# Talking-heads attention in float32: scores mixed whole instead of in parts, the second mixing matrix scaled on GpSimd, value products in two bursts a tile

## Chip, core and metric

The kernel runs on one core of a Trainium2 chip, in one launch. TensorE (PE) multiplies into PSUM, VectorE (DVE), ScalarE (ACT) and GpSimd (POOL) do elementwise work, and SyncE (SP) issues nearly all the DMAs. The five run their own instruction streams in order and meet at semaphores. The metric is device time in microseconds (us) of one execution, lower is better; the number of a kernel is the median of its runs.

## What is computed

Attention over 4 batches, 12 heads, 448 tokens and 64 features a head, in which the heads are mixed before and after the softmax, then a gated feed-forward layer and a top-1 mixture of eight experts. All is float32. The change touches the attention alone:

```python
scores = scale * np.matmul(q, k.transpose(0, 1, 3, 2))
scores = np.einsum('bhij,hg->bgij', scores, w_pre)
scores = scores - np.max(scores, axis=-1, keepdims=True)
attn = np.exp(scores)
attn = attn / (np.sum(attn, axis=-1, keepdims=True) + 1e-09)
attn = np.einsum('bhij,hg->bgij', attn, w_post)
return np.matmul(attn, v)
# then the gated layer and the experts on the tokens' rows
```

## The kernel before

The attention has 16 tiles, four of 110, 110, 110 and 120 query rows for each batch. A tile is cut into blocks of ten query rows, 11 or 12 to a tile and 180 in all. A block holds ten rows of twelve heads, so 120 partitions, with 448 keys along each. The main loop in `attention` makes one turn a block, from n = -8 on, and in each turn every stage works on another block. Per block the stages are:

- `fetch` (L233): two DMAs on SP gather the block's rows out of the tile's scores S into `xm`, eight turns ahead.
- `high` and `low` (L241, L248): `xm` is split into two float32r parts, `xh` (rounded, mostly on DVE) and the rest (mostly on POOL, at 27 blocks on DVE). The first ten blocks (`NATIVE`) are not split.
- `premix` (L254): PE mixes the heads of the block, in three float32r products (L260 to L262), or in one full float32 product for the first ten (L257). PSUM tile `psm`, three buffers.
- `peak` (L264): DVE takes each row's negated maximum `nm` (L267), ACT the exponential `e` and its row sums (L270).
- `norm` (L273): DVE adds a small number to the sums (L276), inverts them (L279) and scales the second mixing matrix K2 by them, which gives `kk` (L282).
- `post` (L286): PE mixes the weights, four full float32 products with `e` as weights and `kk` streamed (L290), into `pso`, two buffers.
- `evac` (L293): ACT (in one turn of 45 DVE) copies `pso` to the tile's weights `AT` (L298).

Between these lie, in the same turns, the scores of the next tile (`qk`, twelve heads a tile, two float32r products each, L230, copied out of PSUM by ACT at L231), the products of the last tile's weights with the values (`av`, L301: twelve halves a tile, spread by the table `AV` over nine of its turns, L318; two halves are sixteen instructions in the trace, and DVE copies the result out at L320), and the low parts of queries and keys on POOL (L204).

Beside the attention, `conv_steps` rounds the float64 weights of the gated layer to float32 for later: 72 pieces of 128x384, each with a load `f` (L123), five DVE steps (L134, L137, L140, L144, L149), one addition on POOL (L127) and a store (L146). `convert` spreads these steps evenly over the turns: 0.41 pieces a turn.

A full float32 product stands in the trace as two PE instructions and a float32r product as one. The order on each engine is the order of the code (`manual_schedule`). The gated layer starts on PE when the attention's products are through.

Of the kernel before, what the change touches and what calls it, by code (L numbers as in the profile page):

```python
"""Talking-heads attention, a gated feed-forward layer and a top-1 mixture of experts, one launch.

Large float32 products run as single-pass products of float32r parts (x = hi + lo, 12 bits each), the others in full;
the float64 weights come in as their bits and are rounded to float32 on the chip.
"""
# [6 lines left out]
F32 = mybir.dt.float32  # L12
F32R = mybir.dt.float32r
# [10 lines left out]
U = 448                      # tokens of a unit of the gated layer  # L24
CAP = 264                    # rows of an expert in the static part; the rest goes through a loop
TS = CAP // 3
OVB = 12                     # blocks of 128 rows that an expert may have beyond CAP
STR = -(-(CAP + 128 * OVB) // 16) * 16   # rows of an expert in the routing table
ITS = [(0, 110, 11), (110, 110, 11), (220, 110, 11), (328, 120, 12)]  # query rows: start, count, blocks
ORDERED = {mybir.EngineType.PE, mybir.EngineType.DVE, mybir.EngineType.Activation, mybir.EngineType.Pool, mybir.EngineType.SP}  # L30
# The attention's turns: a block of ten query rows enters in each and passes a stage in each. A batch has 45.
TURNS = 45
LA, HA, LO = 8, 6, 5         # turns that a block is fetched ahead, and its two parts made ahead, of its last stage
NATIVE = 10                  # blocks that are mixed in full float32, while the parts' engines prepare the keys
HIGH_ACT, HIGH_LAST = (35, 40), 186   # turns of a batch, and all from the last on, whose high parts ScalarE makes
LOW_DVE = (9, 18, 21, 25, 26, 33, 39)   # turns whose low parts VectorE makes
OPER_DVE = (27, 30, 37, 38, 41)   # turns in which VectorE makes a low part of the queries or keys
EVAC_DVE = (10,)             # turns in which VectorE takes the mixed weights out of PSUM
QK = [0, 1, 2, 3, 3, 5, 5, 6, 7, 8, 9, 10]   # turn of a tile's fetches in which a head of the next tile is multiplied
QK0 = [2, 2, 4, 4, 4, 5, 5, 5, 6, 6, 6, 7]   # the same for the first tile  # L40
QL = [0, 3, 6, 7]            # turns in which the queries after those are loaded
QL0 = [4, 6, 7, 8]
KL = [21, 23, 24, 29, 31, 35]   # turns of a batch in which the next one's keys are loaded
K0 = [1, 6, 7, 9]            # turns in which the first batch's later keys are prepared
VL = [(0, 7), (0, 9), (0, 9), (0, 9)]   # tile and turn of a batch's last stages in which its values are loaded
V0 = [4, 5, 9, 16]
AV = [1, 1, 2, 2, 3, 5, 6, 6, 7, 7, 9, 10]   # turns in which the last tile's weights are multiplied with the values
LGS = [2] * 12 + [4, 4]      # how the logits of a unit are spread over the products of the next
AHEAD = 3                    # tiles of weights that are loaded ahead
LOW_W = {0} | {k for k in range(200) if k % 3 == 2 and not 18 < k < 72}   # tiles of weights whose low parts VectorE makes  # L50
PARTS = ((3, 7), (4, 7), (5, 7))   # an expert's second products after which a part of its rows goes out
GATHER = [2, 2, 1, 1, 0, 0]  # chunks of the next expert's rows that are transposed beside them
CV = 384                     # elements a partition of a piece of the float64 conversion


# ------------------------------------------------------------------ host layout
# [53 lines left out]
# ------------------------------------------------------------------ float64 bits -> float32  # L110
def conv_steps(nc, pool, wx, wf):
    """Generator: rounds CV x 128 float64 numbers at a time to float32 (to nearest even), in five steps."""
# [5 lines left out]
    for i in range(len(spots) + 2):  # L118
# [9 lines left out]
        if now:  # L128
            lo, hi = raw[i - 1][:, :, 0], raw[i - 1][:, :, 1]
            a = pool.tile([128, CV], U32, name="cva", bufs=3)  # L130
            e = pool.tile([128, CV], U32, name="cve", bufs=2)
            ef = e.bitcast(F32)
            # The high word as a float32 times 2^-112 has the float32 exponent three places to the right.
            V.tensor_scalar(out=a.bitcast(F32), in0=hi.bitcast(F32), scalar1=2.0 ** -112, scalar2=None, op0=ALU.mult)  # L134
# [19 lines left out]
# ------------------------------------------------------------------ attention  # L154
def attention(tc, qa, ka, qt, kt, vt, k1, k2, xT, wx, wf):
    nc = tc.nc
    with ExitStack() as ctx:
        P = pools(tc, ctx)
        kr, kp, qr, qp, sp, cst, vp, xm, xs, ep, at, sm, xo, cv = (P(n, b) for n, b in (
            ("kr", 3), ("kp", 6), ("qr", 4), ("qp", 4), ("sp", 4), ("acst", 1), ("vp", 7), ("xm", 6), ("xs", 4), ("ep", 3), ("at", 2), ("asm", 4), ("xo", 1), ("cv", 2)))  # L160
# [4 lines left out]
        K1H = cst.tile([120, 120], F32R, name="K1H")  # L165
        K1L = cst.tile([120, 120], F32R, name="K1L")
# [7 lines left out]
        def load_k(b, g):  # L174
            if b:
                r = kr.tile([128, 2, S], F32, name="kraw")
            else:                # where a tile's weights go later
                r = spare[:, 2 * g * S:2 * g * S + 2 * S].rearrange("p (h s) -> p h s", s=S)
            RAW["k", b, g] = r
            nc.sync.dma_start(out=r, in_=kt[b, :, 2 * g:2 * g + 2, :])  # L180
# [6 lines left out]
        def prep_k(b, g):       # heads 2g, 2g + 1: hi in the upper 64 rows, lo in the lower  # L187
# [12 lines left out]
        def oper_low():         # a low part that waits, a turn after its high part at the earliest  # L200
            n = now["n"]
            if LATER and LATER[0][0] <= n:
                _, c, r, a = LATER.pop(0)
                (nc.vector if n % TURNS in OPER_DVE else nc.gpsimd).tensor_tensor(out=c, in0=r, in1=a.bitcast(F32), op=ALU.subtract)  # L204

        def prep_q(t, hf):      # three heads: hi and lo, twice
# [34 lines left out]
        def high(n):  # L241
            if n < NATIVE:
                return
            a = xs.tile([120, S], F32R, name="xh")
            (nc.scalar.copy if n % TURNS in HIGH_ACT or n >= HIGH_LAST else nc.vector.tensor_copy)(a, XS[n])  # L245
            XS[n] = a, XS[n]

        def low(n):  # L248
            if n < NATIVE:
                return  # L250
            a, x = XS[n]
            (nc.vector if n % TURNS in LOW_DVE else nc.gpsimd).tensor_tensor(out=x.bitcast(F32R), in0=x, in1=a.bitcast(F32), op=ALU.subtract)  # L252

        def premix(n):  # L254
            ps = PS[n] = pm.tile([120, 512], F32, name="psm")
            if n < NATIVE:
                nc.tensor.matmul(ps[:, :S], K1, XS.pop(n), start=True, stop=True)  # L257
                return
            a, x = XS.pop(n)
            nc.tensor.matmul(ps[:, :S], K1H, a, start=True, stop=False)  # L260
            nc.tensor.matmul(ps[:, :S], K1L, a, start=False, stop=False)
            nc.tensor.matmul(ps[:, :S], K1H, x.bitcast(F32R), start=False, stop=True)  # L262

# [9 lines left out]
        def norm(n):  # L273
# [8 lines left out]
            nc.vector.tensor_scalar(out=kk, in0=K2, scalar1=r2, scalar2=None, op0=ALU.mult)  # L282
# [19 lines left out]
        def av(t, k):           # half k of twelve: two of the four row chunks of two heads  # L302
# [30 lines left out]
        # ---- the first two tiles' scores: full float32, the other head's rows times zeros  # L333
# [16 lines left out]
        cold = ep.tile([120, S], F32, name="e")     # a product of zeros, for the clock  # L350
# [14 lines left out]
        nc.scalar.copy(K1H, K1)  # L365
        nc.vector.tensor_tensor(out=K1L, in0=K1, in1=K1H.bitcast(F32), op=ALU.subtract)

        # ---- one block a turn, its stages in different turns
        for n in range(-LA, N + 1):
# [22 lines left out]
            if 0 <= n + 3 < N:  # L392
                premix(n + 3)
            scale = norm(n + 1) if 0 <= n + 1 < N else iter(())
            next(scale, None)
            if 0 <= n + 2 < N:
                peak(n + 2)
            if 0 <= n + LO < N:
                low(n + LO)
# [5 lines left out]
            if 0 <= n + HA < N:  # L405
                high(n + HA)
# [22 lines left out]
# ------------------------------------------------------------------ the two feed-forward layers  # L429
def feed_forward(tc, xT, wf, wg, wt, w1, w2, cs, out, x2, tab, keep):  # L430
    nc = tc.nc
    V = nc.vector
    with ExitStack() as ctx:
# [27 lines left out]
        tk = []                                          # tokens less NT  # L461
# [5 lines left out]
        first = cst.tile([TS, 3], F32, name="first")     # the first expert's tokens  # L467
        V.memset(first, float(NT))
        TB0 = cst.tile([TS, 3], I32, name="TB0")
        RS = cst.tile([112, NE], F32, name="RS")      # sums to the next free row of each expert  # L470
# [33 lines left out]
        def order(inst, earlier):       # on one engine, without a wait  # L504
# [35 lines left out]
        def logits(u, row):     # of a unit that is not the last: on VectorE, beside the next unit's products  # L540
# [317 lines left out]
```

## Time and profile before

| | |
|---|---|
| median of three runs | 1515.37 us (1512.62 to 1516.2) |
| the profiled execution, its span | 1513.0 us |
| first and last product of the post-mixing | 29.7 and 569.0 us |
| PE, DVE, ACT, POOL busy over the span | 91%, 71%, 45%, 61% |

The attention takes the first 575 us or so and the two feed-forward layers the rest. The span is the profiled execution's own time; it lies 2.4 us under the median. Busy shares over the whole span mix the attention, where DVE has hardly a gap, with the later layers, where PE has none, so each stage has to be read by itself.

### The profile page before, as it was taken

How to read it: one execution, taken by the hardware profiler on the slowest of the kernel's cores; microseconds unless marked ns; L12 is line 12 of the kernel's file. 1: busy time of each engine (PE TensorE's matmuls, PEld its weight loads, DVE VectorE, ACT ScalarE, POOL GpSimd, SP SyncE). 2: the span in 40 equal slices, each digit the busy share in tenths (PEclk: the TensorE clock that was granted, in tenths of full speed). 3: DMA queues.
4: the chain of work that ended last, by engine and by line, in shares of the span. 5: the costliest groups of instructions: out<-in, count | busy, mean ns of one | idle time of the engine just before them, and what ended most of it. 6: DMA issues, size and time to landing. Idle time of an engine off the chain costs nothing.

```text
span 1513.0 us, 25664 instructions
## 1 busy us (share of the span) xinstructions
PE 1377.2 (91%) x9270; PEld 1210.4 (80%) x9270; DVE 1066.8 (71%) x2055; ACT 675.8 (45%) x1282; POOL 918.5 (61%) x560
## 2 busy tenths in 40 slices
PE   8788997998889988999999998999898799999996
PEld 3666776776667777998888897889787699999995
DVE  4899999999999997861995199529957333333331
ACT  4566666565566554333223222322331345555541
POOL 4666677766767556564557545754563566666661
PEclk9999999999999999999999999999998899999998
DMA  7675686568667666533324332333233466656650
GB/s 245 206 219 180 192 262 202 179 194 241 209 185 223 186 209 210 179 129 134 103 101 135 111 104 103 129 108 108 94 104 102 131 201 214 207 188 208 205 181 20
DMA packets 106840, 251.30 MB, mean 166 GB/s; under 512 B 28190, under 2 KB 71294, under 8 KB 106592
## 3 DMA queue, kind: packets, MB, share of 16 engines
q1 hardware_dynamic: 102351, 237.54, 49.0%
q0 software_dynamic: 4352, 12.02, 2.7%
q8 instruction: 76, 1.25, 0.3%
q14 instruction: 61, 0.49, 0.1%
HBM read 180.00 MB, written 31.79 MB: 140 GB/s over the span
## 4 chain that ended last, share of the span: by engine, by line
PE 41%; DVE 40%; issue 9%; DMA 5%; ACT 2%; SPq 2%; POOL 1%; DVEq 0%; POOLq 0%; ACTq 0%
PE mm L502 11%; PE mm L500 11%; PE mm L501 11%; DVE e L634 6%; DVE junk L546 6%; DVE kk L282 5%; DVE nm L267 4%; DVE xh L245 3%; DMA f<-in_wx 2%; DVE cva L134 2%; PE pso L290 2%; DVE e L633 1%; DVE e L636 1%; DVE e L635 1%; DVE cve L137 1%
## 5 line engine op out<-in xcount | busy, mean ns | idle before, releaser
L490 POOL TENSOR_TENSOR wlo<-wraw,whi 128x1536 fp32r<-128x1536 f32 x108 | 383.3, 3549 | 197.8 <-ACT whi L488 181.4
L500 PE MATMUL mm<-xhi,whi 128*128 128x448 f32 (+1 forms) x960 | 325.4, 339 | 12.9 <-DVE e L635 11.1
L502 PE MATMUL mm<-xlo,whi 128*128 128x448 f32 (+1 forms) x960 | 321.5, 335 | 2.5 <-POOL xlo L521 2.5
L501 PE MATMUL mm<-xhi,wlo 128*128 128x448 f32 (+1 forms) x960 | 321.2, 335 | 0.0
L290 PEld LDWEIGHTS pso<-kk,e 120*112 120x112 f32 x1440 | 168.6, 179 | 89.5 <-ACT AT L298 49.4
L290 PE MATMUL pso<-kk,e 120*112 120x120 f32 x1440 | 186.7, 273 | 50.6 <-DVE kk L282 20.0
L488 ACT CAST whi<-wraw 128x1536 fp32r<-128x1536 f32 x136 | 200.9, 1477 | 62.2 <-PE mm L502 47.6
L500 PE MATMUL mm<-hhi,whi 128*128 128x264 f32 (+1 forms) x672 | 221.9, 330 | 7.1 <-ACT hhi L639 7.1
L252 POOL TENSOR_TENSOR xm<-xm,xh 120x448 fp32r<-120x448 f32 x143 | 180.1, 1260 | 78.4 <-DVE xh L245 49.5
L502 PE MATMUL mm<-hlo,whi 128*128 128x264 f32 (+1 forms) x672 | 219.2, 326 | 1.7 <-POOL hlo L640 1.7
L501 PE MATMUL mm<-hhi,wlo 128*128 128x264 f32 (+1 forms) x672 | 218.0, 324 | 0.0
L270 ACT ACTIVATE e<-psm,nm 120x448 f32<-120x448 f32 x180 | 114.4, 635 | 204.8 <-DVE r L279 167.6
L500 PEld LDWEIGHTS mm<-xhi,whi 128*128 128x128 f32 x960 | 181.5, 189 | 26.7 <-DVE e L635 15.3
L502 PEld LDWEIGHTS mm<-xlo,whi 128*128 128x128 f32 x960 | 181.4, 189 | 12.7 <-POOL xlo L521 3.7
L501 PEld LDWEIGHTS mm<-xhi,wlo 128*128 128x128 f32 x960 | 181.9, 189 | 9.0 <-issue 0.2
L634 DVE RECIPROCAL e<-e 128x448 f32<-128x448 f32 x48 | 141.4, 2946 | 0.7
L500 PEld LDWEIGHTS mm<-hhi,whi 128*128 128x128 f32 x672 | 129.2, 192 | 12.9 <-ACT hhi L639 8.2
L502 PEld LDWEIGHTS mm<-hlo,whi 128*128 128x128 f32 x672 | 129.1, 192 | 8.5 <-POOL hlo L640 3.5
L546 DVE CUSTOM_DVE_ANT_0 junk<-row,WT 112x768 f32<-112x768 f32 x96 | 135.0, 1406 | 0.9 <-ACT row L536 0.7
L640 POOL TENSOR_TENSOR hlo<-e,hhi 128x448 fp32r<-128x448 f32 x48 | 66.8, 1393 | 111.0 <-ACT hhi L639 111.0
L501 PEld LDWEIGHTS mm<-hhi,wlo 128*128 128x128 f32 x672 | 129.2, 192 | 4.8
L267 DVE TENSOR_REDUCE nm<-psm 120x1 f32<-120x448 f32 x180 | 109.5, 608 | 1.1 <-PE psm L257 1.1
(138 smaller groups left out, 2383.4 us busy)
## 6 DMA issues: line engine op xcount, KB each, us to landing
wraw<-wf SPq DMA_DIRECT2D x72, 768.0 KB
wraw<-in_w SPq DMA_DIRECT2D x64, 768.0 KB
xm<-S SPq DMA_DIRECT2D x360, 105.0 KB
f<-in_wx SPq DMA_DIRECT2D x72, 384.0 KB
wf<-cva SPq DMA_DIRECT2D x72, 192.0 KB
qraw<-in_qt SPq DMA_DIRECT2D x56, 180.0 KB
kraw<-in_kt SPq DMA_DIRECT2D x18, 448.0 KB
vt<-in_vt SPq DMA_DIRECT2D x16, 336.0 KB
```

Source lines behind the costliest of these rows:

```text
L252: (nc.vector if n % TURNS in LOW_DVE else nc.gpsimd).tensor_tensor(out=x.bitcast(F32R), in0=x, in1=a.bitcast(F32), op=ALU.subtract)
L267: nc.vector.tensor_reduce(out=nm, in_=ps[:, :S], axis=AX.X, op=ALU.max, negate=True)
L270: nc.scalar.activation(e, ps[:, :S], AF.Exp, bias=nm, scale=1.0, accum_out=su)
L282: nc.vector.tensor_scalar(out=kk, in0=K2, scalar1=r2, scalar2=None, op0=ALU.mult)
L290: nc.tensor.matmul(po[:, c, :120], e[:, 112 * c:112 * c + 112], kk, start=True, stop=True)
L488: nc.scalar.copy(a, r)
L490: eng.tensor_tensor(out=b, in0=r, in1=a.bitcast(F32), op=ALU.subtract)
L500: nc.tensor.matmul(ps, w[0][:, j, :], x[0], start=first, stop=False)
L501: nc.tensor.matmul(ps, w[1][:, j, :], x[0], start=False, stop=False)
L502: nc.tensor.matmul(ps, w[0][:, j, :], x[1], start=False, stop=last)
L546: V.tensor_tensor_reduce(out=jk, in0=row[j], in1=WT[:, e, :], scale=1.0, scalar=0.0, op0=ALU.mult, op1=ALU.add, accum_out=lg[:, j, e:e + 1])
L634: V.reciprocal(out=e, in_=e)
```

## The change

- `high`, `low`, the matrices `K1H` and `K1L` and the pool `xs` are gone. `premix` is one full float32 product for all 180 blocks.
- `kk` is made on GpSimd, with a second multiplication by 1.0.
- The low parts of queries and keys are all on GpSimd (`OPER_DVE` is gone; it had put six halves of keys on DVE).
- `EVAC_DVE` has four turns of 45 instead of one: 16 copies of `pso` on DVE in place of 4.
- The stages are further apart: `premix` four turns ahead of `post` (three before), `peak` three (two) and `norm` two (one). The pool of `e` has five buffers (three), that of the small tiles five (four).
- `AV` puts the value products of a tile into two turns, six halves in each.

All other lines of the diff are comments and blank lines.

```diff
-LA, HA, LO = 8, 6, 5
-NATIVE = 10
-HIGH_ACT, HIGH_LAST = (35, 40), 186
-LOW_DVE = (9, 18, 21, 25, 26, 33, 39)
-OPER_DVE = (27, 30, 37, 38, 41)
-EVAC_DVE = (10,)
+LA = 8
+MIX, PEAK, NORM = 4, 3, 2
+EVAC_DVE = (2, 10, 21, 32)
...
-AV = [1, 1, 2, 2, 3, 5, 6, 6, 7, 7, 9, 10]
+AV = [3] * 6 + [8] * 6
...
-                (nc.vector if n % TURNS in OPER_DVE else nc.gpsimd).tensor_tensor(out=c, in0=r, in1=a.bitcast(F32), op=ALU.subtract)
+                nc.gpsimd.tensor_tensor(out=c, in0=r, in1=a.bitcast(F32), op=ALU.subtract)
...
-            if n < NATIVE:
-                nc.tensor.matmul(ps[:, :S], K1, XS.pop(n), start=True, stop=True)
-                return
-            a, x = XS.pop(n)
-            nc.tensor.matmul(ps[:, :S], K1H, a, start=True, stop=False)
-            nc.tensor.matmul(ps[:, :S], K1L, a, start=False, stop=False)
-            nc.tensor.matmul(ps[:, :S], K1H, x.bitcast(F32R), start=False, stop=True)
+            nc.tensor.matmul(ps[:, :S], K1, XS.pop(n), start=True, stop=True)
...
-            nc.vector.tensor_scalar(out=kk, in0=K2, scalar1=r2, scalar2=None, op0=ALU.mult)
+            nc.gpsimd.tensor_scalar(out=kk, in0=K2, scalar1=r2, scalar2=1.0, op0=ALU.mult, op1=ALU.mult)
...
-            if 0 <= n + 3 < N:
-                premix(n + 3)
-            scale = norm(n + 1) if 0 <= n + 1 < N else iter(())
+            if 0 <= n + MIX < N:
+                premix(n + MIX)
+            scale = norm(n + NORM) if 0 <= n + NORM < N else iter(())
             next(scale, None)
-            if 0 <= n + 2 < N:
-                peak(n + 2)
-            if 0 <= n + LO < N:
-                low(n + LO)
+            if 0 <= n + PEAK < N:
+                peak(n + PEAK)
...
-            if 0 <= n + HA < N:
-                high(n + HA)
```

Lines move: L257 becomes L238, L290 L266, L318 L294, L267 L243, L282 L258, L298 L274, and the conversion's DVE steps L131, L134, L137, L141 and L146.

DVE in the middle of the attention, one turn and part of the next, before (`r` are the sums, then their inverse, `X` the value products on their way out):

```order
L276 TENSOR_SCALAR r_5600<-su 120x1
L267 TENSOR_REDUCE nm<-psm 120x1
L279 RECIPROCAL r_5608<-r_5600 120x1
L137 TENSOR_SCALAR cve<-cva 128x384
L282 TENSOR_SCALAR kk<-K_123,r_5608 120x120
L245 CAST xh<-xm 120x448
L320 COPY X<-psv 128x3x11x10
L140 TENSOR_SCALAR cva<-cva 128x384
```

And two turns with the same kind of steps in the changed kernel:

```order
L252 TENSOR_SCALAR r_5668<-su 120x1
L243 TENSOR_REDUCE nm<-psm 120x1
L255 RECIPROCAL r_5675<-r_5668 120x1
L134 TENSOR_SCALAR cve<-cva 128x384
L137 TENSOR_SCALAR cva<-cva 128x384
L252 TENSOR_SCALAR r_5696<-su 120x1
L243 TENSOR_REDUCE nm<-psm 120x1
L255 RECIPROCAL r_5703<-r_5696 120x1
L141 SCALAR_TENSOR_TENSOR cva<-f_5464,cve 128x384
```

Two DVE instructions of each turn (`kk`, `xh`) are gone. POOL at a like place, before:

```order
L127 TENSOR_TENSOR cve<-cva,cve 128x384
L204 TENSOR_TENSOR qlo<-qraw,qhi 128x360
L252 TENSOR_TENSOR xm<-xm,xh 120x448
L204 TENSOR_TENSOR qlo<-qraw,qhi 128x360
L252 TENSOR_TENSOR xm<-xm,xh 120x448
```

and in the changed kernel:

```order
L258 TENSOR_SCALAR kk<-K_120,r_3653 120x120
L124 TENSOR_TENSOR cve<-cva,cve 128x384
L199 TENSOR_TENSOR qlo<-qraw,qhi 128x360
L258 TENSOR_SCALAR kk<-K_120,r_3697 120x120
L258 TENSOR_SCALAR kk<-K_120,r_3727 120x120
L124 TENSOR_TENSOR cve<-cva,cve 128x384
```

Where a subtraction of 448 elements a partition stood, a scaling of 120 stands, and it waits for DVE's `r`. PE around value products, before:

```order
L290 MATMUL pso<-kk,e 112x120 x4
L318 MATMUL psv<-AT,vt 64x120 x4
L260 MATMUL psm<-xh,K1H 120x448
L261 MATMUL psm<-xh,K1L 120x448
L262 MATMUL psm<-xm,K1H 120x448
L230 MATMUL psq<-ks,qhi 110x448
L230 MATMUL psq<-ks,qlo 110x448
```

and in the changed kernel, a turn without value products, one with a burst and one after it:

```order
L238 MATMUL psm<-xm,K_119 120x448
L266 MATMUL pso<-kk,e 112x120 x4
L294 MATMUL psv<-AT,vt 64x110 x24
L238 MATMUL psm<-xm,K_119 120x448
L225 MATMUL psq<-ks,qhi 110x448
L225 MATMUL psq<-ks,qlo 110x448
L266 MATMUL pso<-kk,e 112x120 x4
```

One premix product stands for three, and 24 value products stand in a row.

## Rows read from the trace of the kernel before

**Rows 1.** The page: busy time of the engines, and DVE's busy tenths in 40 slices.

```profile
PE 1377.2 (91%) x9270; PEld 1210.4 (80%) x9270; DVE 1066.8 (71%) x2055; ACT 675.8 (45%) x1282; POOL 918.5 (61%) x560
...
DVE  4899999999999997861995199529957333333331
```

**Rows 2.** Busy time of each engine in a stretch, then clock, DMA share and rate.

```profile
100.00:508.00 408.00, 357.83 (x2873) 287.47 (x2872) 403.60 (x980) 248.75 (x601) 284.30 (x240) 0.99 0.68 207
```

**Rows 3.** The post-mixing's line L290: durations in ns, first and last start.

```profile
L290 PE MATMUL pso<-kk,e x1440: 263/266/514, 29.7 to 569.0; 120*112 120x120 f32 x180
```

**Rows 4.** DVE's groups in 100 to 508 us: count, busy us, mean ns, idle before.

```profile
L282 DVE TENSOR_SCALAR kk<-K,r 120x120 f32<-120x120 f32 x132 | 77.3, 586 | 0.0
L245 DVE CAST xh<-xm 120x448 fp32r<-120x448 f32 x126 | 64.9, 515 | 0.8 <-DMA xm<-S 0.7
...
L252 DVE TENSOR_TENSOR xm<-xm,xh 120x448 fp32r<-120x448 f32 x19 | 15.5, 814 | 0.0
```

**Rows 5.** The timeline of all engines around 305 us: start, duration, what.

```profile
302.80 0.27 DVE L282 TENSOR_SCALAR kk<-K,r 120x120 f32<-120x120 f32 x1
...
302.98 0.38 DVE L245 CAST xh<-xm 120x448 fp32r<-120x448 f32 x1
...
305.61 1.27 POOL L252 TENSOR_TENSOR xm<-xm,xh 120x448 fp32r<-120x448 f32 x1
...
305.79 1.17 DVE L282 TENSOR_SCALAR kk<-K,r 120x120 f32<-120x120 f32 x1
```

**Rows 6.** DVE's timeline late in the attention: two conversion steps.

```profile
562.46 0.34 DVE L137 TENSOR_SCALAR cve<-cva 128x384 uint32<-128x384 uint32 x1
...
563.84 0.54 DVE L144 SCALAR_TENSOR_TENSOR cva<-f,cve 128x384 uint32<-128x384 uint32 x1
```

**Rows 7.** PE's timeline at five places; what follows directly gives the spacing.

```profile
24.31 0.92 PE L257 MATMUL psm<-xm,K 120*120 120x448 f32 x2
25.06 2.54 PE L226 MATMUL psq<-AT 128*110 128x448 f32 x6
...
305.79 0.47 PE L260 MATMUL psm<-xh,K1H 120*120 120x448 f32 x1
...
306.50 0.37 PE L230 MATMUL psq<-ks,qhi 128*110 128x448 f32 x1
306.70 0.36 PE L230 MATMUL psq<-ks,qlo 128*110 128x448 f32 x1
307.10 1.05 PE L290 MATMUL pso<-kk,e 120*112 120x120 f32 x8
307.91 0.44 PE L260 MATMUL psm<-xh,K1H 120*120 120x448 f32 x1
...
569.97 2.68 PE L318 MATMUL psv<-AT,vt 112*64 112x120 f32 x48 [0.24 <-ACT AT L298]
572.48 2.63 PE L318 MATMUL pso<-AT,vt 112*64 112x120 f32 x48
```

**Rows 8.** POOL's groups in 100 to 508 us, as rows 4.

```profile
L252 POOL TENSOR_TENSOR xm<-xm,xh 120x448 fp32r<-120x448 f32 x114 | 144.0, 1264 | 57.4 <-DVE xh L245 39.5 <-issue 8.3 <-ACT xh L245 3.6
L127 POOL TENSOR_TENSOR cve<-cva,cve 128x384 f32<-128x384 f32 x54 | 61.9, 1146 | 25.9 <-DVE cve L149 17.6 <-PE psm L262 3.6 <-DVE r L276 3.0
...
L204 POOL TENSOR_TENSOR ks<-kraw,ks 64x448 fp32r<-64x448 f32 x26 | 32.3, 1247 | 1.7
```

**Rows 9.** SP from 100 to 508 us: the fetches, one other issue, its longest wait.

```profile
L238 SPq DMA_DIRECT2D xm<-S x266: 762/783/1183, 100.7 to 506.9; - x133
...
317.98 0.49 SPq L123 DMA_DIRECT2D f<-in_wx  x1
...
SPq L146 <- DVE r L276: 53.4, 30, 4.3
```

**Rows 10.** PE's timeline in the first turns: two premix products, two turns apart.

```profile
40.49 0.92 PE L257 MATMUL psm<-xm,K 120*120 120x448 f32 x2
...
44.86 0.92 PE L257 MATMUL psm<-xm,K 120*120 120x448 f32 x2
```

More of the change, by code (lines that the diff above doesn't have):

```diff
@@ L158, in attention @@
         P = pools(tc, ctx)
-        kr, kp, qr, qp, sp, cst, vp, xm, xs, ep, at, sm, xo, cv = (P(n, b) for n, b in (
-            ("kr", 3), ("kp", 6), ("qr", 4), ("qp", 4), ("sp", 4), ("acst", 1), ("vp", 7), ("xm", 6), ("xs", 4), ("ep", 3), ("at", 2), ("asm", 4), ("xo", 1), ("cv", 2)))
+        kr, kp, qr, qp, sp, cst, vp, xm, ep, at, sm, xo, cv = (P(n, b) for n, b in (
+            ("kr", 3), ("kp", 6), ("qr", 4), ("qp", 4), ("sp", 4), ("acst", 1), ("vp", 7), ("xm", 6), ("ep", 5), ("at", 2), ("asm", 5), ("xo", 1), ("cv", 2)))
         pq, pm, pp, pv = (P(n, b, "p") for n, b in (("pq", 2), ("pm", 3), ("pp", 2), ("pv", 1)))
@@ L164, in attention @@
         K2 = cst.tile([120, 120], F32, name="K2")
-        K1H = cst.tile([120, 120], F32R, name="K1H")
-        K1L = cst.tile([120, 120], F32R, name="K1L")
         conv = conv_steps(nc, cv, wx, wf)
@@ L239, in fetch @@
             XS[n] = x
-        def high(n):
-            if n < NATIVE:
-                return
[L244 to L252, printed above, removed]
         def premix(n):
             ps = PS[n] = pm.tile([120, 512], F32, name="psm")
-            if n < NATIVE:
-                nc.tensor.matmul(ps[:, :S], K1, XS.pop(n), start=True, stop=True)
-                return
-            a, x = XS.pop(n)
-            nc.tensor.matmul(ps[:, :S], K1H, a, start=True, stop=False)
-            nc.tensor.matmul(ps[:, :S], K1L, a, start=False, stop=False)
-            nc.tensor.matmul(ps[:, :S], K1H, x.bitcast(F32R), start=False, stop=True)
+            nc.tensor.matmul(ps[:, :S], K1, XS.pop(n), start=True, stop=True)
         def peak(n):
@@ L364, in attention @@
         nc.vector.tensor_scalar(out=K1, in0=K1, scalar1=1.0 / np.sqrt(D), scalar2=None, op0=ALU.mult)
-        nc.scalar.copy(K1H, K1)
-        nc.vector.tensor_tensor(out=K1L, in0=K1, in1=K1H.bitcast(F32), op=ALU.subtract)
         for n in range(-LA, N + 1):
```

## The prediction

> **What bounds the kernel now.** I read the page first. Over the whole span PE is busiest, but DVE's tenths stand at 9 for the first 14 slices and fall afterwards [rows 1], so the attention, where the change is made, has to be read alone. From 100 to 508 us DVE is busy 403.60 of 408 us, PE 357.83, POOL 284.30 and ACT 248.75 [rows 2]. SP issues 266 fetches there [rows 9], two a block, so 133 turns pass in 408 us: **3.07 us a turn**. PE's 357.83 is less full than it looks, because a product's duration holds its latency: in rows that follow without a wait the spacing is shorter than the duration [rows 7]. The limit is DVE. DVE's groups have next to no idle time before them [rows 4].
>
> Part of DVE's time isn't its own work. A scaling `kk` takes 0.27 us alone, but 1.17 us at 305.79 us, where a POOL subtraction has begun 0.18 us earlier: the subtraction ends at 306.88 us, `kk` at 306.96 us [rows 5]. The mean of `kk` is 586 ns and that of `xh` 515 ns against 0.38 us alone [rows 4, 5].
>
> The Trainium skill has the rule for this in "SBUF — State Buffer", section "Who interferes with whom": VectorE and GpSimd share one pair of ports, as an exclusive lock for the whole instruction, and whichever starts first blocks the other. The trace agrees in the pair just read. It is weighed below, since the change gives GpSimd a new instruction a turn.
>
> **The change part by part.** *DVE* loses `kk`, `xh` and its share of the low parts: 77.3 + 64.9 + 15.5 = 157.7 us in the middle stretch [rows 4], 1.19 us a turn. It gains twelve copies of `pso` in the whole attention, which I price like the cast of about as many elements at 0.5 us [rows 4]: 6 us, 4 of them in the middle. What is left is 403.6 - 157.7 + 4 = 250 us, **1.88 us a turn**, with the stretching of the conversion steps as it is now. Six halves of keys go from DVE to POOL, at 1.25 us each [rows 8]: 8 us.
>
> *PE* in spacings: the three-part premix takes 306.50 - 305.79 = 0.71 us, the full one 25.06 - 24.31 = 0.75 us; a turn's post-mixing 307.91 - 307.10 = 0.81 us; a score product 0.20 us; 48 value instructions in a row 572.48 - 569.97 = 2.51 us [rows 7]. A tile has 11.25 turns on average, 24 score products and two such bursts. The new turn is 0.75 + 0.81 + 24 x 0.20 / 11.25 (0.43) + 2 x 2.51 / 11.25 (0.45) = **2.44 us**. The premix by itself is 0.04 us a turn dearer, 7 us in all, and it is hidden as long as PE isn't the limit; after the change PE is.
>
> *SP*: two fetches of 783 ns, and beside them 0.41 loads and 0.41 stores of the conversion, and 106 loads and stores of queries, keys, values and results over 180 turns, at up to 0.49 us [rows 9]: 1.57 + 1.41 x 0.49 = **2.26 us a turn**, with no gap between them. The change removes none of it. SP waits long now for DVE before a conversion store, 53.4 us in 30 times [rows 9]; the fetches of the next turns stand behind that wait. A fetch now has four turns to land before its premix (before, two to its split), so a late one is forgiven more.
>
> *ACT* has 248.75 / 133 = 1.87 us a turn [rows 2] and loses the twelve copies and a few casts. *POOL* loses 144.0 us of subtractions [rows 8] and keeps 284.30 - 144.0 = 140.3 us, with the keys' halves 1.1 us a turn. It gains `kk`, of which the trace has no POOL row. The nearest rows by kind of work are the conversion's addition, 384 elements a partition in 1146 ns, and the keys' subtraction, 448 in 1247 ns [rows 8]; in proportion 120 elements are 0.36 us, and if a small instruction costs as much as the dearest row, 1.25 us. I take 0.4 us, since those two rows grow with the elements. POOL then has 1.5 us a turn. `post` needs `kk` two turns after its sums instead of one, so this stays off PE's path.
>
> *What is late next.* PE (2.44) and SP (2.26) lie close together, DVE and ACT 0.5 us below. PE doesn't reach its sum, since the engines meet every turn. The first turns show by how much: they already mix in full float32, have no `xh` and no value products yet. There PE's sum is 0.75 + 0.81 + 0.43 = 1.99 us, and the premix products at 40.49 and 44.86 us, two turns apart, give 2.19 us a turn [rows 10], 10% more. With that, 2.44 becomes 2.65 us. The middle saves 133 x (3.07 - 2.65) = **56 us**. From 29.7 to 569.0 us are 539 us [rows 3], so 47 turns lie outside the middle, in 131 us, 2.79 each. Ten of them are native already and gain little; the last 20 or so have no scores to make, and PE's sum there is near 2.0. I take 2.5 on average: **13 us**. The further stage costs one more premix before the first post-mixing, 1 us. Together 68 us: 1513.0 - 68 = 1445 us. The median of the runs shown is 2.4 us above that span, so **1447 us**. The later layers do the same work and move forward with the attention's end.
>
> **Rivals.** *PE runs full* at 2.44 us, because DVE and the further stages leave enough slack: the middle saves 84, the ends 20, and the time is 1411 us. Against it: the 10% in the first turns.
>
> *SP becomes the limit.* It issues in order, and its waits for DVE, 0.4 us a turn now, may remain, since the conversion's store still stands between the fetches. With gaps and some transfers later (the DMA share of 0.68 [rows 2] grows to 0.79 at 2.65 us a turn), 2.85 us a turn: 29 us in the middle, 6 at the ends, 1480 us. For it: a sum of 2.26 us leaves little room; against it: DVE reaches the store's step earlier.
>
> *The bursts starve the others.* During 2.51 us of value products no premix comes, and with three `psm` buffers DVE and ACT can't work far ahead. If DVE then needs 2.4 us in the 9.25 turns without a burst and the two burst turns last 2.0 + 2.5 us, a tile is 31.2 us, 2.77 a turn: 40 + 9 us saved, 1466 us. Speaking against it: DVE's 1.88 us is below PE's 2.0 in such a turn.
>
> *Slower: `kk` on GpSimd costs too much.* POOL's instructions and those of DVE that stretch beside them go partly one after the other. Before, they add up to 284.30 / 133 = 2.14 for POOL [rows 2], 0.27 and 0.36 for `kk` and `xh` alone [rows 5], and 0.41 x (3 x 0.34 + 2 x 0.54) = 0.86 for the five conversion steps [rows 6]: 3.63 us in a turn of 3.07, so 0.85 of the sum is what a turn takes. After, it is 0.85 x (1.1 + 0.86 + k) for a `kk` of k: 2.0 us at 0.4, 2.7 at 1.25, and 3.07 from k = **1.65 us** on. Beyond that the kernel is slower; at 2.0 us, which a two-step scaling with a scalar for each partition could cost, a turn is 3.37 and 180 turns are 54 us more, 1569 us. The dearest small POOL row, 1.25 us, doesn't reach the point.
>
> By the skill's rule above with no overlap at all, the sum itself would be the turn, and the point would lie at 1.1 us. The rows of before, 3.63 in 3.07, don't go so far, so I give the rule's full form a small part of the chance.
>
> **How the numbers follow.** Forecast 1447 us, with 1430 to 1460 as its own spread: 0.54. PE full, 1411: 0.13. Bursts, 1466: 0.11. SP, 1480: 0.13. `kk` at about its point, within 0.3% of now (that is about what a measurement of this kernel can tell from no change): 0.04. `kk` beyond it, 1569: 0.05. Faster is 0.91, same 0.04, slower 0.05. The range leaves out the slower and unchanged cases and the lower part of the first rival: **1415 to 1487 us**.
>
> **What would show it.** Right: premix at 0.75 us spacing in the middle, 2.6 to 2.7 us a turn, DVE with idle time before its `nm` because of PE, ACT's waits for DVE mostly gone, POOL's `kk` below 0.7 us. SP as the limit would show as fetches issued without a gap and DVE idle for `f` or PE for `xm`. Wrong would be a DVE still without idle time, or PE waiting for `kk` from POOL.

## The result, and the profile after

The changed kernel takes **1464.36 us** (median of four runs, 1461.21 to 1466.73), the kernel before on the same chip 1515.78 us: a ratio of 0.9662 with an interval of 0.9645 to 0.9679. The time is 51 us shorter, where 68 were forecast. It lies in the range of 1415 to 1487 us, 17 us above the forecast of 1447 and outside its own spread, and next to the rival in which the bursts starve the other engines (1466).

The profiled execution has a span of 1460.5 us, 52.5 less than before. Its page first: busy time by engine, and DVE's busy tenths in 40 slices.

```profile
PE 1361.3 (93%) x9100; PEld 1182.2 (81%) x9100; DVE 873.4 (60%) x1691; ACT 663.4 (45%) x1261; POOL 834.7 (57%) x603
...
DVE  3767767757666778709990799169937333333331
```

In the attention DVE stood at 9 from the third slice on [rows 1] and now stands at 5 to 7. The post-mixing's line (durations in ns, first and last start):

```profile
L266 PE MATMUL pso<-kk,e x1440: 263/266/513, 33.9 to 518.9; 120*112 120x120 f32 x180
```

And the middle of the attention, with PE, PEld, DVE, ACT and POOL busy, granted clock, DMA share and rate:

```profile
100.00:460.00 360.00, 336.59 (x2645) 257.98 (x2642) 243.44 (x686) 233.67 (x575) 206.18 (x257) 0.98 0.76 228
```

The groups of DVE and POOL in the same stretch (count, busy us, mean ns, idle before and what ended it) hold 129 `nm` and 129 `kk`, so 129 turns in 360 us, 2.79 us a turn in place of 3.07:

```profile
L243 DVE TENSOR_REDUCE nm<-psm 120x1 f32<-120x448 f32 x129 | 79.0, 612 | 0.0
L296 DVE COPY X<-psv 128x330 f32<-128x330 f32 (+1 forms) x23 | 17.4, 757 | 55.0 <-PE psv L294 54.9
L258 POOL TENSOR_SCALAR kk<-K,r 120x120 f32<-120x120 f32 x129 | 74.4, 577 | 107.9 <-DVE r L255 86.4 <-PE psq L225 17.4 <-PE psm L238 1.3
```

The difference between the two spans can be split by stage, with the 47 turns outside the middle taken as what is left over. The first post-mixing comes 4.2 us later (33.9 for 29.7). From there to the last one 539.3 us have become 485.0: 133 turns at 2.79 in place of 3.07 save 36.8 us, and the other 47 take 485.0 - 371.2 = 113.8 us in place of 131.3, 17.5 less. What follows the last post-mixing is 1460.5 - 518.9 = 941.6 us, before 944.0: 2.4 us. Together 36.8 + 17.5 - 4.2 + 2.4 = 52.5.

DVE no longer sets the pace: 243.44 of 360 us. These waits of that stretch bear on what does (who waited, for whom, us, times, longest; the last row is from SP's own list).

```profile
ACT e L246 <- DVE r L255: 86.9, 62, 5.3
DVE X L296 <- PE psv L294: 54.9, 22, 5.9
DVE cva L131 <- DMA f<-in_wx: 49.8, 30, 5.1
PE psm L238 <- DMA xm<-S: 9.3, 4, 3.1
SPq L143 <- DVE r L252: 10.3, 7, 3.8
```

Three things that the forecast's sum didn't have stand in the timelines. The first is a burst. PE, then DVE (start, duration, instruction):

```profile
169.06 0.92 PE L238 MATMUL psm<-xm,K 120*120 120x448 f32 x2
169.81 0.98 PE L266 MATMUL pso<-kk,e 120*112 120x120 f32 x8
173.11 2.68 PE L294 MATMUL psv<-AT,vt 112*64 112x120 f32 x48
175.72 1.01 PE L238 MATMUL psm<-xm,K 120*120 120x448 f32 x2
```

```profile
171.33 0.53 DVE L146 SCALAR_TENSOR_TENSOR cve<-f,cve 128x384 f32<-128x384 uint32 x1
175.84 0.79 DVE L296 COPY X<-psv 128x360 f32<-128x360 f32 x1 [3.98 <-PE psv L294]
176.79 0.61 DVE L243 TENSOR_REDUCE nm<-psm 120x1 f32<-120x448 f32 x1
```

The copy of the value products is the next instruction in DVE's order. DVE stands before it for 3.98 us, until the burst that begins at 173.11 us is done, and `nm` stands behind it, and so do the exponentials that need it.

The second comes in the turn of a batch's first value products. Before them PE waits 2.64 us for the fetch of a later block, and soon after that its products take about twice as long. PE's timeline, and the engines' busy time with the granted clock, 0.51 from 191 to 198 us, so nearly all of it at the lower level, 1.2 GHz:

```profile
189.69 1.01 PE L238 MATMUL psm<-xm,K 120*120 120x448 f32 x2 [2.64 <-DMA xm<-S]
...
191.90 1.91 PE L266 MATMUL pso<-kk,e 120*112 120x120 f32 x8 [0.78 <-POOL qlo L199]
193.74 4.54 PE L294 MATMUL psv<-AT,vt 112*64 112x110 f32 x48
198.21 1.01 PE L238 MATMUL psm<-xm,K 120*120 120x448 f32 x2
```

```profile
184.00:191.00 7.00, 4.36 (x24) 2.83 (x24) 2.24 (x8) 2.87 (x8) 2.09 (x3) 1.00 0.90 273
191.00:198.00 7.00, 6.22 (x55) 5.91 (x56) 2.59 (x6) 2.83 (x8) 2.62 (x4) 0.51 0.82 261
```

The third is the start: with one more premix ahead of the first post-mixing, PE meets a premix whose fetch hasn't landed while the next score products stand behind it, waits 3.83 us, and goes on at a granted clock of 0.63.

```profile
20.61 1.82 PE L238 MATMUL psm<-xm,K 120*120 120x448 f32 x2 [3.83 <-DMA xm<-S]
22.22 3.33 PE L221 MATMUL psq<-AT 128*110 128x448 f32 x6
```

```profile
21.00:25.00 4.00, 4.00 (x7) 1.53 (x7) 1.16 (x2) 0.75 (x2) 2.68 (x2) 0.63 0.46 128
```

### The profile page after: what moved, and what is told of

Same layout as the page of the kernel before. It is cut to its first block, busy times and chain, and to the rows that moved or that the text cites. A ratio compares the mean times of both kernels' runs of the same rounds, so it can differ in the third digit from the quotient of the medians.

```text
span 1460.5 us, 24833 instructions
## 1 busy us (share of the span) xinstructions
PE 1361.3 (93%) x9100; PEld 1182.2 (81%) x9100; DVE 873.4 (60%) x1691; ACT 663.4 (45%) x1261; POOL 834.7 (57%) x603
## 4 chain that ended last, share of the span: by engine, by line
PE 59%; DVE 19%; DMA 8%; issue 6%; ACT 2%; POOL 2%; SPq 2%; POOLq 0%; DVEq 0%; ACTq 0%
PE mm L472 12%; PE mm L470 12%; PE mm L471 12%; PE pso L266 6%; DVE e L604 6%; PE psm L238 6%; DVE junk L516 5%; DMA f<-in_wx 4%; PE psv L294 4%; PE psq L225 3%; DVE e L603 1%; SPq L233 1%; DVE e L606 1%; DMA xm<-S 1%; DVE e L605 1%
## 5 line engine op out<-in xcount | busy, mean ns | idle before, releaser
L266 PEld LDWEIGHTS pso<-kk,e 120*112 120x112 f32 x1440 | 172.1, 179 | 55.7 <-POOL kk L258 22.0
L266 PE MATMUL pso<-kk,e 120*112 120x120 f32 x1440 | 183.3, 271 | 20.0 <-ACT AT L274 9.8
L258 POOL TENSOR_SCALAR kk<-K,r 120x120 f32<-120x120 f32 x180 | 104.0, 578 | 158.1 <-DVE r L255 124.0
L238 PE MATMUL psm<-xm,K 120*120 120x448 f32 x360 | 169.9, 554 | 13.1 <-DMA xm<-S 13.1
```

The costliest lines, as they stand in the source:

```text
L258: nc.gpsimd.tensor_scalar(out=kk, in0=K2, scalar1=r2, scalar2=1.0, op0=ALU.mult, op1=ALU.mult)
L266: nc.tensor.matmul(po[:, c, :120], e[:, 112 * c:112 * c + 112], kk, start=True, stop=True)
```

## Experiments

Two questions were put. Which of the edits carries the gain? And what holds the turn at 2.79 us and the start 4 us back? The ratio of each kernel is to the kernel before, run on the same chip (its median 1514.9 to 1517.6 us).

### Which edit carries the gain

**The full float32 mixing alone**, in the kernel before: all other edits of the change are left out.

```diff
-NATIVE = 10
+NATIVE = 180
```

> The kernel before with one part of the change alone: all blocks mixed in full float32, with no parts made; kk stays on VectorE, stages and value products as before. Theory A (this part carries the gain): VectorE falls from 3.03 to about 2.3 us a turn, 1470 to 1480 us. Theory B (it takes kk's move as well): 1495 us or more, VectorE still without idle time.

Measured: 1454.39 us (1453.51 to 1460.37), ratio 0.9600 [0.9572, 0.9628]. One line gives more than the whole change, by 10 us, and more than either theory gave it. Its middle, and DVE's scaling there:

```profile
100.00:460.00 360.00, 352.93 (x2701) 264.82 (x2696) 267.81 (x829) 242.27 (x590) 129.27 (x123) 1.00 0.76 231
```

```profile
L282 DVE TENSOR_SCALAR kk<-K,r 120x120 f32<-120x120 f32 x132 | 51.0, 386 | 0.0
```

132 turns in 360 us, 2.73 us each. DVE keeps `kk` and is busy 268 of 360 us all the same: without `xh` and the subtractions on POOL, `kk` has gone from 586 ns [rows 4] to 386. PE is nearly full.

**`kk` on GpSimd alone**, in the kernel before.

```diff
-            nc.vector.tensor_scalar(out=kk, in0=K2, scalar1=r2, scalar2=None, op0=ALU.mult)
+            nc.gpsimd.tensor_scalar(out=kk, in0=K2, scalar1=r2, scalar2=1.0, op0=ALU.mult, op1=ALU.mult)
```

> The kernel before with one part of the change alone: kk on GpSimd. Theory A (VectorE's own work was the limit, so each instruction taken off it counts): VectorE loses 0.58 us a turn, 1440 to 1470 us. Theory B (VectorE and GpSimd go partly one after the other, and GpSimd's subtractions are still there): the sum of both is as before, 0.27 us off one and about 0.6 us onto the other, 1505 to 1525 us. Theory C (the post-mixing one turn after its kk is too near): slower than 1525 us.

Measured: 1514.82 us (1511.95 to 1518.15), ratio 1.0000 [0.9986, 1.0015]. No change, though DVE loses `kk`, 77.3 us of instructions in 408 us [rows 4]. DVE's busy time from 100 to 460 us falls from 356.3 to 337.5 us only. The middle, then the two groups that tell why, and PE's wait:

```profile
100.00:460.00 360.00, 311.47 (x2472) 249.13 (x2472) 337.53 (x736) 219.53 (x529) 327.12 (x327) 0.98 0.67 204
```

```profile
L245 DVE CAST xh<-xm 120x448 fp32r<-120x448 f32 x110 | 89.7, 816 | 1.9 <-DMA xm<-S 1.7
L282 POOL TENSOR_SCALAR kk<-K,r 120x120 f32<-120x120 f32 x115 | 82.8, 720 | 13.4 <-DVE r L279 8.5 <-PE psm L262 1.6 <-PE pso L290 1.2
```

```profile
PE pso L290 <- POOL kk L282: 42.8, 47, 2.2
```

POOL is now busy 327 of 360 us, and the same cast `xh` takes 816 ns where it took 515 [rows 4]. So a good part of what DVE gave up comes back as longer instructions beside a busier POOL, and PE waits for `kk` instead. Not every DVE instruction is stretched: `nm` takes 609 ns here and 608 in the kernel before. That DVE and POOL together bounded the kernel before fits these rows, but they don't prove it. This kernel keeps the near stages, with `kk` one turn before its use, and 42.8 us of waits for `kk`; `kk` on GpSimd with further stages wasn't run in the kernel before. The 816 ns agree with the rule of the Trainium skill that the prediction weighed ("SBUF — State Buffer", section "Who interferes with whom"): VectorE and GpSimd share a pair of ports, which is locked for a whole instruction. The page limits this to VectorE instructions in its two-port modes or with two inputs in SBUF, a condition that the prediction left out; which mode the cast was in, no run shows.

**`kk` back on DVE**, in the changed kernel, and again in the mended kernel below.

```diff
-            nc.gpsimd.tensor_scalar(out=kk, in0=K2, scalar1=r2, scalar2=1.0, op0=ALU.mult, op1=ALU.mult)
+            nc.vector.tensor_scalar(out=kk, in0=K2, scalar1=r2, scalar2=None, op0=ALU.mult)
```

> The changed kernel with kk back on VectorE, all else as changed. Theory A (the full float32 mixing alone frees VectorE far enough; the scaling's move is worth little): VectorE goes from 243.4 / 129 = 1.89 to about 2.3 us a turn, still under PE's 2.47, and the time stays within 6 us of the changed kernel's 1464, with kk at a mean below 0.4 us because GpSimd no longer runs 1.25 us subtractions beside it. Theory B (the scaling's move is what carries the gain): VectorE is near its limit again, 1485 us or more, and PE waits for kk from DVE.

Measured: 1465.22 us (1464.68 to 1466.07), ratio 0.9675 [0.9647, 0.9704]: the same as with `kk` on GpSimd. The mean of `kk` on DVE is above what was expected, 451 ns, and costs nothing that shows, since DVE has room (270 of 360 us).

> The three mended, with kk back on VectorE. With the bursts' stall in place kk's place made no difference (1465 against 1464). Theory A (VectorE has room at 2.3 us a turn even when PE runs at 2.5): within 4 us of the three mended. Theory B (nearer to PE's limit the 0.27 to 0.45 us a turn on VectorE count): 5 to 20 us slower.

Measured: 1443.31 us (1439.99 to 1450.32), ratio 0.9513 [0.9489, 0.9538], as the mended kernel with `kk` on GpSimd (0.9532). Three comparisons agree, the first of them with the near stages: the place of `kk` is worth nothing that can be measured.

**The stages as near as before**, in the changed kernel.

```diff
-MIX, PEAK, NORM = 4, 3, 2
+MIX, PEAK, NORM = 3, 2, 1
```

> The changed kernel with the stages three, two and one turn ahead of the post-mixing, as before, instead of four, three and two. Theory A (the further stages give GpSimd its time for kk): PE waits for kk, 10 to 30 us slower than 1464; the start is 4 us earlier. Theory B (the distance isn't needed, as kk takes 0.58 us): the time is 1460, the 4 us of the start gained.

Measured: 1476.24 us (1468.97 to 1477.56), ratio 0.9736 [0.9695, 0.9776], 12 us slower than the change. PE's wait for `kk`, here and in the changed kernel:

```profile
PE pso L266 <- POOL kk L258: 21.3, 21, 4.4
```

```profile
PE pso L266 <- POOL kk L258: 0.9, 1, 0.9
```

The further stages are worth their later start here, where `kk` is on GpSimd and the values come in bursts. The kernel with the mixing alone has them near, `kk` on DVE and the values spread, and it is faster; which of its differences makes the distance needless wasn't tried apart. Nor were the copies of `pso` that went to DVE and the low parts that went to POOL.

### What holds the turn at 2.79 us

**The values spread again**, in the changed kernel.

```diff
-AV = [3] * 6 + [8] * 6
+AV = [1, 1, 2, 2, 3, 5, 6, 6, 7, 7, 9, 10]
```

> The changed kernel with the value products spread over nine turns of a tile as before. Theory A (bursts are cheaper on PE, 0.052 against about 0.065 us an instruction with their joints, and what VectorE waits for them is slack): 8 to 15 us slower than 1464. Theory B (the bursts starve VectorE, whose copy of the results waits 54.9 us for them between 100 and 460 us): 8 to 20 us faster, and VectorE's wait at that copy falls under 15 us.

Measured: 1450.74 us (1443.05 to 1454.13), ratio 0.9586 [0.9556, 0.9616], 14 us faster than with bursts by the medians, 12 by the ratios, as the second theory had it. But DVE's wait for the value products falls only to 41.4 us, less far than expected:

```profile
100.00:460.00 360.00, 357.60 (x2769) 269.96 (x2768) 251.43 (x713) 243.06 (x595) 213.14 (x264) 1.00 0.77 235
```

```profile
L296 DVE COPY X<-psv 128x330 f32<-128x330 f32 (+1 forms) x24 | 18.2, 758 | 41.5 <-PE psv L294 41.4
```

PE has hardly a gap, 357.60 of 360 us, at 134 turns, 2.69 us each. So values spread over the turns leave no gaps but make the turn's own work on PE dearer than the 2.44 us of the sum, which was made with values in a row; rows of this are shown with the mended kernel with spread values below.

**The copy of the value products a turn later**, in the changed kernel: the burst stays; DVE's copy and its store are emitted in the next turn, behind the maximum.

```diff
-                nc.vector.tensor_copy(out=X[:, j - 2:j + 1, :n]...
-            if k == 11:
-                ...
+                def out(X=X, pa=pa):
+                    nc.vector.tensor_copy(out=X[:, j - 2:j + 1, :n]...
+                    if k == 11:
+                        ...
+                av_ps["out"] = out
...
             next(scale, None)
+            av_ps.pop("out", int)()
```

> The changed kernel with VectorE's copy of a burst's results, and their store, put one turn later, behind that turn's maximum. Theory A (a burst costs time because VectorE, in order, stands at that copy until the burst is through, and the next blocks' maxima stand behind it): the copy's wait falls from 54.9 to under 15 us between 100 and 460 us, and the time is 1448 to 1456 us, near the kernel with spread value products. Theory B (a burst keeps PE from the next premix, so VectorE has nothing to work on either way): the wait moves to the maximum, and the time stays within 4 us of 1464.

Measured: 1446.37 us (1441.87 to 1450.61), ratio 0.9549 [0.9514, 0.9584], 18 us faster than the change. The time is that of the theory that blames the place of the copy, though the wait has fallen to 29.1 us and not to under 15.

```profile
L297 DVE COPY X<-psv 128x330 f32<-128x330 f32 (+1 forms) x24 | 18.1, 755 | 29.1 <-PE psv L294 29.1
L243 DVE TENSOR_REDUCE nm<-psm 120x1 f32<-120x448 f32 x136 | 83.3, 612 | 0.8 <-PE psm L238 0.8
```

136 turns in 360 us, 2.65 us each, with the same bursts and the same three `psm` buffers. So what the bursts cost did not come through the buffers, and most likely came through an instruction at the head of DVE's order. One rival is left: the edit moves the results' store too, and SP's wait before it falls from 18.1 us to 5.9. Since PE's waits for fetches fall only from 9.3 us to 6.1, that can be a small part at most, but the copy wasn't moved without its store.

**The next batch's values loaded one at a time**, in the changed kernel: the table names for each of four loads the tile and turn of a batch.

```diff
-VL = [(0, 7), (0, 9), (0, 9), (0, 9)]
+VL = [(0, 1), (0, 4), (0, 6), (0, 9)]
```

> The changed kernel with the four loads of a batch's values at turns 1, 4, 6 and 9 of the batch's first tile instead of 7, 9, 9 and 9. Theory A (the three loads in a row, 1 MB, delay the fetches behind them, and PE's waits of 2.6 to 3.2 us for xm at 187, 312 and 442 us, with the half clock after two of them, come from that): the second tile of a batch goes from 3.26 (3.25, 2.96) to below 2.9 us a turn and the time is 1450 to 1456 us. Theory B (the fetches are late for another reason, such as the wait for the results' store in front of them): within 4 us of 1464.

Measured: 1450.18 us (1447.6 to 1452.33), ratio 0.9574 [0.9547, 0.9602], 14 us faster than the change. In SP's timeline of the changed kernel three loads stand in a row ahead of a fetch:

```profile
180.60 1.36 SPq L211 DMA_DIRECT2D vt<-in_vt  x3
182.48 1.65 SPq L233 DMA_DIRECT2D xm<-S  x2
```

The fetch comes late, and PE waits as shown above. SP had also stood before the results' store until 176.66 us, when DVE's copy was done. PE's wait for `xm` in this kernel, from 100 to 460 us (9.3 us in four times in the changed kernel):

```profile
PE psm L238 <- DMA xm<-S: 1.8, 2, 1.3
```

Two stretches with a batch's loads, in the changed kernel and then in this one (columns as above):

```profile
150.00:200.00 50.00, 45.82 (x349) 35.92 (x348) 30.57 (x89) 28.19 (x71) 22.80 (x31) 0.93 0.76 230
...
300.00:350.00 50.00, 45.78 (x346) 35.75 (x344) 30.28 (x85) 31.47 (x75) 28.77 (x35) 0.93 0.81 246
```

```profile
150.00:200.00 50.00, 47.31 (x374) 36.08 (x373) 33.88 (x98) 32.52 (x82) 23.98 (x34) 1.00 0.81 250
...
300.00:350.00 50.00, 44.45 (x357) 33.81 (x357) 31.38 (x92) 33.25 (x79) 31.13 (x38) 1.00 0.81 249
```

The clock stays at its upper level now. The timeline of the changed kernel prices one occurrence. A burst of the same size at the upper clock takes 211.53 - 209.12 = 2.41 us:

```profile
209.12 2.48 PE L294 MATMUL psv<-AT,vt 112*64 112x110 f32 x48
211.53 1.01 PE L238 MATMUL psm<-xm,K 120*120 120x448 f32 x2
```

So there are 2.64 us of waiting, a burst of 198.21 - 193.74 = 4.47 us for 2.41, and a post-mixing of 193.74 - 191.90 = 1.84 us for 0.81, together 5.7 us. The two stretches at 0.93 are 11 us by that, and the other two waits, up to 9.3 - 2 x 2.64 = 4 us, come on top: near the 14 by the medians (13 by the ratios). The loads in a row don't do it alone: the kernel with spread values has the same loads, and there PE is busy 357.60 of the 360 us at a granted clock of 1.00. Whether the fetch is late because SP issues it behind the loads or because the transfers share the DMA engines wasn't tried apart.

**The first scores ahead of the waiting premix**, in the changed kernel.

```diff
-QK0 = [2, 2, 4, 4, 4, 5, 5, 5, 6, 6, 6, 7]
+QK0 = [2, 2, 3, 3, 3, 5, 5, 5, 6, 6, 6, 7]
```

> The changed kernel with three of the first tile's score products moved ahead of the first premix. Theory A (at the start PE stands 3.83 us before the first premix, which the change put before these products, until the first block has been fetched): the products fill that wait, the first post-mixing starts at 30 to 31 us instead of 33.9, and the time is 1460 us. Theory B (the products wait for ScalarE's copies, so nothing is filled): 1464 us.

Measured: 1456.23 us (1453.66 to 1464.76), ratio 0.9634 [0.9594, 0.9673], 8 us by the medians and 4 by the ratios, where 4 were expected, with intervals that overlap. The start itself is shown by PE's timeline: the first post-mixing starts at 30.57 us, where the changed kernel's starts at 33.9, and PE's wait for the fetch is 0.80 us for 3.83.

```profile
20.30 0.98 PE L238 MATMUL psm<-xm,K 120*120 120x448 f32 x2 [0.80 <-DMA xm<-S]
...
30.57 0.98 PE L266 MATMUL pso<-kk,e 120*112 120x120 f32 x8
```

### All three mended, and what is left

**The late copy, the early values and the early scores together** (the last three diffs).

> The changed kernel with the late copy, the earlier value loads and the three score products ahead of the first premix together. If the three are separate stalls (18, 14 and 8 us alone), 1424 to 1432 us, PE near its full spacing of 2.5 us a turn in the middle and no wait of PE for xm over 1.5 us. If they are the same stall seen three times, 1440 to 1447 us.

Measured: 1444.88 us (1442.23 to 1449.69), ratio 0.9532 [0.9509, 0.9555]. The three give 20 us together, where alone they give 18, 14 and 8: about half of what they fill is the same slack.

```profile
L266 PE MATMUL pso<-kk,e x1440: 263/266/424, 32.7 to 492.9; 120*112 120x120 f32 x180
```

```profile
L131 DVE TENSOR_SCALAR cva<-f 128x384 f32<-128x384 f32 x57 | 30.5, 535 | 77.0 <-DMA f<-in_wx 59.0 <-DMA xm<-S 10.8 <-DMA wf<-cva 6.1
```

The attention ends 26 us earlier than the changed kernel's, but the span, 1440.4 us, is only 20 us shorter: 947.5 us follow the last post-mixing in place of 941.6. Part of these six go where the gated layer starts, since PE is busy 15.1 of the first 20 us there, 17.9 in the changed kernel. This isn't where the three overlap: the kernel with the late copy alone has 947.9 us behind its last post-mixing. Alone the three bring that post-mixing forward by 22, 11 and 7 us, together by 26, so they overlap in the attention. Two of the 14 us that don't add up are lost at its start, where the first post-mixing begins at 32.7 us and not at 30.57.

**The mended kernel with spread values** (the diff of the spread above).

> The one before with the value products spread over nine turns. Theory A (with VectorE no longer standing at the copy, bursts are only the cheaper form for PE, by the joints between the kinds of products, about 0.13 us a turn): 8 to 20 us slower than the kernel with the three mended, PE without a gap at 2.62 us a turn. Theory B (bursts still hold up the other engines): the same or faster.

Measured: 1446.52 us (1443.18 to 1448.32), ratio 0.9530 [0.9508, 0.9553]: the same as with bursts, where a loss of 8 to 20 us was expected. That expectation missed.

```profile
100.00:460.00 360.00, 358.00 (x2770) 270.19 (x2769) 258.32 (x715) 245.65 (x595) 209.78 (x264) 1.00 0.78 235
```

Here PE has hardly a gap at 134 turns, 2.69 us. In the mended kernel with bursts PE has 346 of 360 us and 137 turns, 2.63 us. PE's timeline late in the attention shows what spreading costs:

```profile
488.34 0.98 PE L266 MATMUL pso<-kk,e 120*112 120x120 f32 x8
489.25 0.60 PE L294 MATMUL psv<-AT,vt 112*64 112x110 f32 x8
489.78 1.01 PE L238 MATMUL psm<-xm,K 120*120 120x448 f32 x2
490.63 0.98 PE L266 MATMUL pso<-kk,e 120*112 120x120 f32 x8
```

With values between them the post-mixing takes 0.91 us for 0.81 and the premix 0.85 for 0.75, and eight value instructions take 0.53 us, where eight of a burst's 48 take 0.40. Sixteen take 0.91 us. Eight turns of a tile hold values (not nine), four of them sixteen instructions, so a turn is 0.75 + 0.81 + 0.43 + 8 x 0.20 / 11.25 (0.14) + (4 x 0.91 + 4 x 0.53) / 11.25 (0.51) = 2.64 us on PE: with spread values PE itself all but sets the 2.69. Spread values are dearer on PE and leave no gap; bursts are cheaper and leave gaps; the ends come out alike.

**The float64 pieces loaded one further ahead**, in the mended kernel, against the 59.0 us that DVE waits for `f`.

```diff
-            t = pool.tile([128, CV, 2], U32, name="f64", bufs=3)
-            k, j = spots[i]
-            ...
+        for l in ((0, 1) if i == 0 else (i + 1,)):
+            if l < len(spots):
+                t = pool.tile([128, CV, 2], U32, name="f64", bufs=4)
+                k, j = spots[l]
+                ...
```

> The three mended, and the conversion's float64 pieces loaded one piece further ahead (four buffers). VectorE waits for these loads about 49 us between 100 and 460 us in nearly every kernel. Theory A (that wait is slack, since VectorE has 0.5 us a turn to spare): within 3 us of the three mended, the wait under 10 us and turned into a wait for PE's premix or for the value products. Theory B (the next maximum stands behind it, and PE waits in the end): 5 to 15 us faster.

Measured: 1444.86 us (1436.43 to 1447.06), ratio 0.9516 [0.9492, 0.9541]: the same. The wait for `f` is gone, and DVE waits for others instead, so it was slack:

```profile
L132 DVE TENSOR_SCALAR cva<-f 128x384 f32<-128x384 f32 x57 | 28.3, 496 | 5.5 <-DMA wf<-cva 4.2 <-DMA xm<-S 1.1
L253 DVE TENSOR_SCALAR r<-su 120x1 f32<-120x1 f32 x139 | 20.6, 148 | 38.7 <-ACT e L247 37.9
```

The mended kernel and its three variants lie at 0.951 to 0.953 with intervals that overlap. All four beat both kernels: 1443 to 1447 us against 1464 and 1515.

## Why the prediction was right, and where it was wrong

**What bounded the kernel: right.** The gain comes from taking work off DVE and POOL, and the mixing edit alone brings it all.

**Where the sum missed.** The forecast span was 1445 us and the profiled one is 1460.5. The middle saved 19 us less than forecast and the start cost 3 more; the ends saved 4 more and what follows the attention 2. So the small miss of the total is in part errors that offset each other.

**What was gained by which edit: wrong for `kk`.** The working counted 77.3 us of `kk` among the 157.7 that DVE loses, though it had read that much of this was waiting beside POOL. DVE's sum of 1.88 us a turn came out (243.44 / 129 = 1.89), in part by luck. The working left the conversion's steps as stretched as before, but the five of a piece fell from 3.25 us to 2.79. And it took whole durations off a busy time in which they overlap: from 100 to 460 us before, DVE's durations add up to 423 us in 356 us of busy time. As a cause `kk` was empty: moved alone, with the near stages, it changes nothing, moved back nothing either. The working's pair sum, which counts DVE and POOL together, has it right that this move gains nothing, but it gives 0.85 x (2.14 + 0.36 + 0.86 + 0.72) = 3.47 us a turn with the 0.72 us that `kk` took, where the time stayed as it was. The two engines overlap more than the factor of 0.85 says. (The sum took 0.36 us for `xh` alone, where the row has 0.38 [rows 5]; that changes little.)

**`kk` on GpSimd: right.** 577 ns, between the ends of 0.36 and 1.25 us, nearer to the 0.4 us taken and far from the break-even of 1.65 us. POOL has 206.18 / 129 = 1.60 us a turn (1.5 forecast).

**PE's pieces: right.** The premix spacing is 169.81 - 169.06 = 0.75 us, a burst 175.72 - 173.11 = 2.61 us (2.51 forecast).

**The middle, 2.65 us a turn: the step that failed.** PE's sum was raised by 10%, read from the first turns [rows 10]. (10% on 2.44 us are 2.68 and not 2.65: the middle would have saved 52 us, and the forecast would have been 1451.) Those turns have no value products, so they could not show what a burst does to DVE's order, and they lie before the first three loads in a row. The turn came out 14% above the sum, 2.79 us, and 19 of the 56 us are missing. With the copy a turn later the turn is 2.65 us; the values' loads account for another part of the same slack. The bursts rival had the size right (2.77 us) and the mechanism wrong: it blamed three `psm` buffers, and the late copy removes the cost with the same buffers. That DVE's copy would stand in order before the work behind it could have been read from the code: it is written right behind the burst.

**A late fetch is forgiven more: wrong.** With four turns to land, PE still waits for fetches, 9.3 us in four times, and the lower clock that follows the long ones costs about as much again.

**The start: mis-sized.** One more premix was priced as 1 us. It came before score products in PE's order and the start cost 4.2, of which the reordered start gives back 3.3.

**The ends: mis-sized.** 17.5 us and not 13, at 2.42 us a turn for 2.5.

**SP as the limit: not seen.** Its wait before the conversion's store fell from 53.4 us in 408 [rows 9] to 10.3 in 360, and e.g. the kernel with the late copy has SP carry 136 turns in 360 us.

**ACT's waits for DVE mostly gone: wrong.** They are 86.9 us in 360, where the kernel before had 116.3 in the same stretch. ACT has 1.81 us of work a turn (233.67 / 129), so its waits show only that it isn't the limit.

What stays open: what holds the mended kernels with bursts at 2.6 us a turn, above PE's 2.44, and why three mends fill the same slack.

## What to carry to other kernels

An engine that is busy all the time may be waiting inside its instructions beside another engine (here `kk`, 586 ns before and 386 without the subtractions): count the pair, and try the one edit that takes work from both before those that shift it between them. When a burst is made on one engine, look at what the engines behind it have next in their order: an instruction that waits for the whole burst belongs behind the work that others need. After a limit is lifted, the new one shows first at the seams (a batch's loads in a row, the first turns, the hand-over), so an efficiency read from a quiet stretch is too good for the rest.

## What the runs showed of the hardware

A wait of 2.64 us on PE, with one of 0.78 us soon after it, went with seven microseconds at a granted clock of 0.51, and one of 3.83 us at the start with a stretch at 0.63, in which a premix had 1.61 us to the next instruction (from 20.61 to 22.22) for 0.75. In the first case the low clock cost 2.06 us on the burst and 1.03 on the post-mixing, 3.1 us, a little more than the wait. A scaling of 120x120 by a scalar for each partition takes 577 ns on GpSimd and 720 ns beside the subtractions of the kernel before, against 386 ns on DVE with little work on GpSimd beside it. One full float32 product of 448 columns costs 0.75 us on PE, and three float32r products of the same size 0.71 [rows 7]: the exact form was nearly free there, and what the parts cost was on DVE and POOL.
